# Attention inside a gated mix: three turns a head instead of four, sixteen exponential tiles, v kept 29 columns wide

## The chip, the core and the metric

One core of a Trainium2 chip. The metric is the device time of the whole kernel, in microseconds (us): the median of several runs. A profile of one execution, with every instruction of every engine and its start, comes with it.

## The reference

One block of 2048 tokens, 448 wide, goes through attention with 16 heads of 28 columns and through a gated feed-forward layer, and the two results are mixed by a gate per token. All in float32.

```python
x = A_x
g = _sigmoid((x * gate_w).sum(-1, keepdims=True))
# attention
qkv = (x @ wqkv).reshape(B, S, 3, H, Dh) ...
scores = jnp.einsum("bhqd,bhkd->bhqk", q, k) * (Dh ** -0.5)
p = _softmax(scores, axis=-1)
a = jnp.einsum("bhqk,bhkd->bhqd", p, v) ... @ wo
# feed-forward
b = (_gelu(x @ w_gate) * (x @ w_up)) @ w_down
return g * a + (1 - g) * b
```

S = 2048, D = 448, H = 16, Dh = 28; the hidden width F is 1792.

## The kernel before

**Precision.** A float32 product is taken as three products of parts (hi and lo of each operand, in the format float32r). The contraction over 448 rows so becomes 11 matmuls, the list `PAIRS`. q, k, the projections and the feed-forward layer work in this way; scores stack the parts of q and k on 114 rows, so that one matmul does; values are plain float32, which takes two passes, so that a profile shows two instructions for each.

**Stages.** First q, k, v and the gate's logits. Then attention, which is where the change lies. Then the feed-forward layer ("geglu") with the output projection mixed in.

**Attention.** For a head `h` and a tile `kt` of 128 keys, `scores` (L254) writes two score tiles of 128 keys x 1024 queries, `half` 0 and 1, each by two matmuls of 512 columns, into one of three buffers `sc`; ScalarE takes the exponentials into a tile `pt` of the pool `pp` (L261). `values` (L264) then multiplies v's tile of those keys into `po`: four matmuls of 512 queries, on four strips of 32 columns of TensorE's array side by side, twice for the two passes. `V` holds for each key tile and head 28 columns of v and 4 columns of ones; the first of these gives the sum of the exponentials. When a head is done, `finish` (L273) copies `po` out on VectorE (L275), sends the sums through memory to form reciprocals (L277 to L285), multiplies (L287) and stores (L289).

TensorE doesn't go to the values after every key tile. `ENDS` names the key tiles of a head after which it turns: it then writes `LATE` = 3 more score tiles (of what follows) and after that does the values of all the key tiles gathered. With `ENDS = (3, 7, 11, 15)` a turn has 4 key tiles, so 8 score tiles, and a head has 4 turns.

**Filling.** Between score tiles TensorE works on x @ w_up, and on a part of x @ w_gate, which the next stage will read: the generator `up` (L292) gives one matmul ("product") at a time, 17 weight tiles x 4 blocks of tokens x 11 = 748 in all. A block of 11 gathers in the only buffer `pu`; VectorE copies it to `u` (L307, two buffers), and a DMA stores it in `ud`. `fill(n)` (L315) issues up to n products, and after a block's last one none until two more score tiles are out (`hold`) or until the values have been done. The loop calls it after each score tile but two:

```python
                    if due and count == LATE:
                        for a in due:
                            values(*a)
                        due, hold = [], 0
                    elif count != LATE - 1 or h + kt == 0:
                        first, last = h == 0 and kt <= ENDS[0] + 1, h == H - 1 and kt > ENDS[-2]
                        fill(4 if first or last else RATE)
```

`count` is the number of score tiles since the last turn of `ENDS`, and `RATE` is 2. Products left at the end run in a row behind the last values (L352).

**What sets the order.** All matmuls keep the order in which the program writes them. The other engines' instructions and the DMAs, which all go through SyncE's queue (SP), are put in an order by a planner at compile time; each engine and the queue then work in that order. Semaphores make them wait for their data and for the buffers that they reuse.

**Memory.** `kq` holds Q and K of two heads, even and odd ones in turn. The pool `gp`, with the tiles of w_down (`draw` and `w`, L370 to L374), has room of its own on the other side of the memory from before the attention on, so the first of these tiles are loaded and split while the first heads run. The pools of the last stage (`ap`, `hp`, `tp`, `wpo`) take the addresses that the attention leaves.

Of the kernel before, what the change touches and what calls it, by code (L numbers as in the profile page):

```python
# [7 lines left out]
F32 = mybir.dt.float32  # L8
# [7 lines left out]

S, D, H, DH, F = 2048, 448, 16, 28, 1792
P = 128
TB = 512                 # tokens of a block
NTB = S // TB  # L20
NT = S // P              # token tiles
NKT = S // P             # key tiles
NQK = 2 * D // P         # row tiles of q and k together
NF = F // P              # tiles of the hidden width
FC = 2                   # hidden tiles of a chunk
ENDS = (3, 7, 11, 15)    # key tiles after which TensorE turns from scores to values
LATE = 3                 # score tiles that it writes before it turns
RATE = 2                 # products of x @ w_up, w_gate between score tiles
NB = 3                   # hidden tiles whose x @ w_gate is taken there, too
ORDER = (2, 3, 1, 4, 0, 5, 6)   # chunks of the hidden width  # L30
NR = 4 * DH + 2          # rows of a score product
VW = 450                 # v, the gate's column, a zero column
SCALE = DH ** -0.5
BOUND = 20.0             # scores within +-BOUND need no search for their maximum

# A float32 product is taken as hi*hi + lo*hi + hi*lo, where x = hi + lo exactly and both parts fit
# float32r. The contraction over 448 rows is cut into tiles 0..2 of 128 rows and 64 more rows, whose
# hi and lo parts share one tile. Pairs are (tile of x's parts, tile of the weight's parts).
PAIRS = [(b, w) for b in range(3) for w in (b, 4 + b)] + [(4 + b, b) for b in range(3)] + [(3, 3), (3, 7)]


# [1 line left out]
def gated_mix(ctx: ExitStack, tc: tile.TileContext, xT, wqk, wvg, wg, wu, wd, wo, sel, ident, out):  # L43
    nc = tc.nc

    def mm(o, lhsT, rhs, start, stop):
        tc.keep_in_program_order(nc.tensor.matmul(o, lhsT, rhs, start=start, stop=stop))  # L47

    dram = ctx.enter_context(tc.tile_pool(name="dram", bufs=1, space=DRAM))
    qkd = dram.tile([2, 2 * D, S], F32, name="qkd")      # hi, lo of q's and k's rows  # L50
    shd = dram.tile([H, 2, S], F32, name="shd")          # hi, lo of minus the rows' shifts
    od = dram.tile([D, S], F32, name="od")                # attention outputs, by head rows
    dend = dram.tile([H, S], F32, name="dend")            # softmax denominators
    rdend = dram.tile([H, S], F32, name="rdend")          # their reciprocals
    ud = dram.tile([NF + NB, P, S], F32, name="ud")       # x @ w_up and some of x @ w_gate

    keep = ctx.enter_context(tc.tile_pool(name="keep", bufs=1))
    X = keep.tile([P, 7, S], F32R, name="X")
    gate = keep.tile([P, 3, NT], F32, name="gate")        # logits, g, 1 - g
    fw = ctx.enter_context(tc.tile_pool(name="fw", bufs=2))  # L60
    attn = ctx.enter_context(ExitStack())
    vp = attn.enter_context(tc.tile_pool(name="vp", bufs=1))
    V = vp.tile([P, NKT, H, 32], F32, name="V")
    kq = attn.enter_context(tc.tile_pool(name="kq", bufs=1))
    heads = [tuple(kq.tile([NR, S], F32R, name=f"{x}{i}") for x in "QK") for i in range(2)]
    for _, K in heads:
        nc.gpsimd.memset(K[96:].bitcast(F32), 1.0)
    nc.gpsimd.memset(V[:, :, :, DH:], 1.0)

# [1 line left out]
    with ExitStack() as ph:  # L71
        wp = ph.enter_context(tc.tile_pool(name="wp", bufs=1))
        st = ph.enter_context(tc.tile_pool(name="st", bufs=2))
# [8 lines left out]

        def raw(src, n=TB):
            t = st.tile([P, TB], F32, name="raw", bufs=6)[:, 0:n]
            nc.sync.dma_start(out=t, in_=src)
# [14 lines left out]
        def load_x(tb):  # L100
            s = slice(tb * TB, (tb + 1) * TB)
            rs = [raw(xT[tb, :, b]) for b in range(4)]
            for b in range(3):
                nc.scalar.activation(X[:, b, s], rs[b], AF.Copy)  # L104
            nc.gpsimd.tensor_copy(X[0:64, 3, s], rs[3][0:64])
            hr = st.tile([P, TB], F32R, name="xhr", bufs=1)
            nc.scalar.activation(hr[64:], rs[3][64:], AF.Copy)
# [5 lines left out]
        def qk_tile(t, tb):  # L113
            s = slice(tb * TB, (tb + 1) * TB)
            p = ps.tile([P, TB], F32, name="pqk")
# [27 lines left out]
            for t in range(NQK):  # L143
                qk_tile(t, tb)

        # |q.k| <= (sum of q's squared maxima + sum of k's) / 2, by head
        sq = wp.tile([P, NQK], F32, name="sq")
        nc.vector.tensor_reduce(sq, mx, axis=AX.X, op=OP.max)
        nc.vector.tensor_tensor(sq, sq, sq, OP.mult)
# [6 lines left out]
        for t in range(NQK):  # L156
            mm(pr[0:1, 0:H], sq[:, t:t + 1], selt[:, t], t == 0, t == NQK - 1)
        for i in range(4, NT):
            v_tile(i)
# [6 lines left out]
        for a in range(2):  # L166
            nc.vector.tensor_copy(sh[:, a, :], hcol[:, a:a + 1].bitcast(F32).to_broadcast([H, P]))
            nc.sync.dma_start(out=shd[:, a].rearrange("h (i n) -> h i n", n=P),
                              in_=sh[:, a:a + 1].to_broadcast([H, NT, P]))
        far = wp.tile([1, 2], F32, name="far")  # L170
# [1 line left out]
        nc.vector.tensor_reduce(far[:, 0:1], pr[0:1, 0:H], axis=AX.X, op=OP.max)  # L172
        nc.vector.tensor_scalar(far[:, 1:2], far[:, 0:1], 2.0 * BOUND / SCALE, None, OP.is_le)
        nc.vector.tensor_copy(flag, far[:, 1:2])
        # g = 1 / (1 + exp(-t))
        nc.scalar.activation(gate[:, 0], gate[:, 0], AF.Exp, scale=-1.0)
        nc.vector.tensor_scalar(gate[:, 0], gate[:, 0], 3e38, 1.0, OP.min, OP.add)  # L177
        nc.vector.reciprocal(gate[:, 1], gate[:, 0])  # L178
# [10 lines left out]
    load_k(heads[0][1], 0)  # L189
    load_q(heads[0][0], 0)  # L190

# [1 line left out]
    bounded = nc.values_load(flag[0:1, 0:1], min_val=0, max_val=1)  # L193
    with tc.If(bounded < 1):
        with ExitStack() as ph:
            gp = ph.enter_context(tc.tile_pool(name="gp", bufs=2))
# [4 lines left out]
            for h in range(H):  # L201
# [5 lines left out]
                for i in range(NT):  # L207
                    p = gps.tile([P, S], F32, name="gsc")
# [11 lines left out]
                nc.sync.dma_start(out=shd[h].rearrange("a (i n) -> i a n", i=NT),  # L220
                                  in_=ms.bitcast(F32))

    gp = ctx.enter_context(tc.tile_pool(name="gp", bufs=1, side="right"))
# [1 line left out]
    halves = {}  # L225

    def load_half(src, f, key, hi):
# [7 lines left out]
    def by_act(o, i):  # L235
        nc.scalar.activation(o, i, AF.Copy)

# [1 line left out]
    with ExitStack() as ph:  # L239
        pp = ph.enter_context(tc.tile_pool(name="pp", bufs=12))  # L240
        op = ph.enter_context(tc.tile_pool(name="op", bufs=2))
        psc = ph.enter_context(tc.tile_pool(name="psc", bufs=3, space=PSUM))
        pso = ph.enter_context(tc.tile_pool(name="pso", bufs=1, space=PSUM))
# [1 line left out]
        PT, PO = {}, {}  # L245
# [18 lines left out]
        def values(h, kt):  # L264
            if kt == 0:
                PO[h] = pso.tile([P, 512], F32, name="po")
            for j in range(4):
                mm(PO[h][j * 32:(j + 1) * 32], V[:, kt, h, :],
                   PT[h, kt, j // 2][:, (j % 2) * 512:(j % 2 + 1) * 512], kt == 0, kt == NKT - 1)
            if kt == NKT - 1:  # L270
                finish(h)
# [18 lines left out]
                                  in_=o[j * 32:j * 32 + DH])  # L290

        def up():  # L292
            # x @ w_up, a product at a time
            todo = [(wu, f, "u") for f in range(NF)] + [(wg, f, "g") for f in range(NB)]
            load_half(*todo[0], nc.vector.tensor_copy)
            for n, (_, f, key) in enumerate(todo):
                for tb in range(NTB):
                    if tb == 1 and n + 1 < len(todo):
                        load_half(*todo[n + 1], nc.vector.tensor_copy)
                    s = slice(tb * TB, (tb + 1) * TB)  # L300
                    p = psu.tile([P, TB], F32, name="pu")
                    for i, (x, w) in enumerate(PAIRS):
                        mm(p, halves[key, f][:, w], X[:, x, s], i == 0, i == len(PAIRS) - 1)
                        if i < len(PAIRS) - 1:
                            yield False
                    u = op.tile([P, TB], F32, name="u")
                    nc.vector.tensor_copy(u, p)  # L307
                    nc.sync.dma_start(out=ud[n, :, s], in_=u)
                    yield True
# [3 lines left out]
        hold = 0  # L313

        def fill(n):  # L315
            # up to n products, and after a block's last none before two more score tiles
            nonlocal hold
            while n and not hold:
                n -= 1
                if next(filler, None):  # L320
                    hold = 2
# [9 lines left out]
        for h in range(H):  # L331
            for kt in range(NKT):
                if kt == 2 and h + 1 < H:
                    load_head(h + 1)
                for half in range(2):
# [6 lines left out]
                    elif count != LATE - 1 or h + kt == 0:  # L342
                        first, last = h == 0 and kt <= ENDS[0] + 1, h == H - 1 and kt > ENDS[-2]
# [9 lines left out]
            pass  # L353
    attn.close()

# [1 line left out]
    with ExitStack() as ph:  # L357
        ap = ph.enter_context(tc.tile_pool(name="ap", bufs=1, reuse_waits="tile"))
        acc = ap.tile([P, NT, D], F32, name="acc")
        hp = ph.enter_context(tc.tile_pool(name="hp", bufs=2, reuse_waits="tile"))  # L360
        tp = ph.enter_context(tc.tile_pool(name="tp", bufs=3, reuse_waits="tile"))
        wpo = ph.enter_context(tc.tile_pool(name="wpo", bufs=1, reuse_waits="tile"))
        psg = ph.enter_context(tc.tile_pool(name="psg", bufs=3, space=PSUM, reuse_waits="tile"))
        psd = ph.enter_context(tc.tile_pool(name="psd", bufs=5, space=PSUM, reuse_waits="tile"))
# [47 lines left out]
                    nc.vector.scalar_tensor_tensor(y, p, g1, acc[:, t], OP.mult, OP.add)  # L412
                    nc.sync.dma_start(out=out[0, t * P:(t + 1) * P], in_=y)

        # the output projection of a block of tokens, mixed in
        WO = wpo.tile([P, 8, D], F32R, name="WO")
        OHL = {}

# [87 lines left out]
```

## Time and profile before

| | us |
|---|---|
| runs, median of 3 (lowest, highest) | 1068.43 (1067.9, 1068.51) |
| profiled execution, span | 1068.0 |
| first stage, to the first scores | 0 to 124 |
| attention, to the last product of the filling | 124 to 777.3 |
| geglu and output projection | 777.3 to 1068.0 |
| TensorE busy, whole span | 1054.2 |
| ScalarE busy, whole span | 616.8 |
| VectorE busy, whole span | 320.2 |

The engines are called PE (TensorE's matmuls), PEld (its weight loads), DVE (VectorE), ACT (ScalarE), POOL (GpSimd) and SP (SyncE, the DMA queue) in the profile's rows. A row of a group has the line of the program, the engine, the operation, what it writes and reads, and a count; then busy time, mean time of one in ns, and idle time before them with what ended it. A row of the timeline has start and length in us, and joins equal instructions that follow each other. All matmuls have line L47, since one helper issues them: `sc`, `po`, `pu`, `pg`, `pd` tell them apart by what they write. A row of a stage's windows has its ends, its length, then busy time and count of PE, PEld, DVE, ACT and POOL, and the clock granted to TensorE (1.00 here).

### The profile page before, as it was taken

The page shows a single profiled execution, that of the slowest core. Times are in us where ns is not written, and L with a number is a line of the kernel's source. Part 1 is how long each engine was busy: PE and PEld are TensorE (multiplying, and loading weights), DVE is VectorE, ACT ScalarE, POOL GpSimd, SP SyncE. Part 2 cuts the span into 40 slices and gives each one's busy share as a digit, 9 for nine tenths or more (in the row PEclk, how much of TensorE's full clock was granted, in tenths as well). Part 3 has the DMA queues.
Part 4 walks back from the last instruction along what each step waited for, and adds up shares of the span by engine and source line. Part 5 has one row for each costly group of instructions (what it writes and reads, how often), then busy time and mean ns, then how long its engine had stood idle before and what let it go on. Part 6 is the DMA issues. An engine that isn't in the chain of part 4 may idle for free.

```text
span 1068.0 us, 14546 instructions
## 1 busy us (share of the span) xinstructions
PE 1054.2 (99%) x5664; PEld 732.2 (69%) x5664; DVE 320.2 (30%) x519; ACT 616.8 (58%) x732; POOL 41.5 (4%) x32
## 2 busy tenths in 40 slices
PE   7999999999999999999999999999999999999998
PEld 5789756556556556556556566565588888888887
DVE  5561111111111111110110110110156656577555
ACT  6322478778777777777777787787643332233321
POOL 5300000000000000000000000000001011100000
PEclk9999999999999999999999999999999999999999
DMA  8875122332332332342332332331164323342233
GB/s 267 291 258 145 57 75 73 120 103 73 102 103 74 98 107 73 94 112 73 94 112 73 93 111 73 94 102 41 64 191 142 99 86 91 95 148 67 63 87 115
DMA packets 58907, 115.85 MB, mean 108 GB/s; under 512 B 12784, under 2 KB 18160, under 8 KB 55216
## 3 DMA queue, kind: packets, MB, share of 16 engines
q1 hardware_dynamic: 58832, 114.85, 35.8%
q8 instruction: 47, 0.77, 0.3%
q14 instruction: 28, 0.23, 0.1%
HBM read 74.44 MB, written 40.37 MB: 108 GB/s over the span
## 4 chain that ended last, share of the span: by engine, by line
PE 88%; DVE 0%; issue 0%; DVEq 0%
PE sc L47 23%; PE po L47 21%; PE pd L47 16%; PE pu L47 16%; PE pg L47 11%; DVE u L307 0%; DVE y L412 0%; DVE gate L178 0%; DVE gate L177 0%; DVE gate L179 0%; DVEq L307 0%
## 5 line engine op out<-in xcount | busy, mean ns | idle before, releaser
L261 ACT ACTIVATE pt<-sc 128x1024 f32<-128x1024 f32 x512 | 482.4, 1026 | 164.6 <-PE sc L47 163.9
L47 PE MATMUL sc<-Q,K 114*128 114x512 f32 x1024 | 317.9, 402 | 1.3 <-issue 1.3
L47 PEld LDWEIGHTS sc<-Q,K 114*128 114x128 f32 x1024 | 188.8, 189 | 94.3 <-issue 54.5
L47 PE MATMUL pu<-X,half 128*128 128x512 f32 x748 | 237.8, 397 | 0.4 <-DVE u L307 0.3
L47 PE MATMUL po<-pt,V 128*32 128x512 f32 x2048 | 233.0, 595 | 0.0
L307 DVE COPY u<-pu 128x512 f32<-128x512 f32 x68 | 47.0, 691 | 491.6 <-PE pu L47 484.7
L47 PEld LDWEIGHTS pu<-X,half 128*128 128x128 f32 x748 | 141.0, 189 | 35.9 <-issue 1.4
L47 PEld LDWEIGHTS po<-pt,V 128*32 128x32 f32 x2048 | 60.0, 109 | 137.8 <-issue 132.2
L47 PE MATMUL pd<-w,hl 128*128 128x448 f32 x672 | 140.9, 366 | 0.0
L47 PEld LDWEIGHTS pd<-w,hl 128*128 128x128 f32 x672 | 126.2, 188 | 12.2
L47 PE MATMUL pg<-X,half 128*128 128x512 f32 x484 | 116.6, 395 | 0.0
L47 PEld LDWEIGHTS pg<-X,half 128*128 128x128 f32 x484 | 90.7, 187 | 20.9
L47 PE MATMUL pqk<-X,WQK 128*128 128x512 f32 x308 | 75.0, 404 | 7.7 <-ACT X L104 6.0
L47 PEld LDWEIGHTS pqk<-X,WQK 128*128 128x128 f32 x308 | 58.6, 192 | 23.7 <-ACT X L104 6.9
L389 ACT ACTIVATE g<-pg 128x512 f32<-128x512 f32 x44 | 26.2, 595 | 78.7 <-PE pg L47 78.6
L390 DVE TENSOR_TENSOR g<-g,u 128x512 f32<-128x512 f32 x56 | 46.0, 830 | 55.0 <-ACT g L389 55.0
L391 ACT ACTIVATE hl<-g 128x512 fp32r<-128x512 f32 x56 | 35.2, 630 | 42.4 <-DVE g L390 36.6
L409 DVE SCALAR_TENSOR_TENSOR acc<-pd,gate,acc 128x448 f32<-128x448 f32 x80 | 53.0, 679 | 6.8 <-PE pd L47 6.8
L437 POOL TENSOR_TENSOR ohl<-oraw,ohl 128x1536 fp32r<-128x1536 f32 x4 | 14.0, 3511 | 752.0 <-DMA u<-ud 749.2
L392 DVE TENSOR_TENSOR hl<-g,hl 128x512 fp32r<-128x512 f32 x56 | 38.3, 687 | 10.6 <-ACT hl L391 8.7
L47 PE MATMUL pd<-WO,ohl 128*128 128x448 f32 x176 | 37.0, 368 | 0.0
L47 PE MATMUL pv<-WV,X 128*128 128x450 f32 x176 | 36.4, 366 | 0.0
(60 smaller groups left out, 325.1 us busy)
## 6 DMA issues: line engine op xcount, KB each, us to landing
ud<-u SPq DMA_DIRECT2D x68, 256.0 KB
qkd<-hl SPq DMA_DIRECT2D x28, 512.0 KB
Q<-qkd SPq DMA_DIRECT2D x64, 224.0 KB
K<-qkd SPq DMA_DIRECT2D x64, 224.0 KB
u<-ud SPq DMA_DIRECT2D x56, 256.0 KB
raw<-in_xT SPq DMA_DIRECT2D x16, 256.0 KB
rb<-rdend SPq DMA_DIRECT2D x64, 64.0 KB
hraw<-in_wu SPq DMA_DIRECT2D x14, 256.0 KB
```

The lines of the kernel that those rows point to most:

```text
L47: tc.keep_in_program_order(nc.tensor.matmul(o, lhsT, rhs, start=start, stop=stop))
L261: nc.scalar.activation(pt, sc, AF.Exp, scale=SCALE)
L307: nc.vector.tensor_copy(u, p)
L389: nc.scalar.activation(g, pg, AF.Gelu_apprx_tanh)
L390: nc.vector.tensor_tensor(g, g, u, OP.mult)
L391: nc.scalar.activation(hl[:, 0], g, AF.Copy)
L392: nc.vector.tensor_tensor(hl[:, 1], g, hl[:, 0].bitcast(F32), OP.subtract)
L409: nc.vector.scalar_tensor_tensor(acc[:, t], p, g1, acc[:, t], OP.mult, OP.add)
L437: nc.gpsimd.tensor_tensor(O[:, 4:7], o[:, 0:3], O[:, 0:3].bitcast(F32), OP.subtract)
```

## The change

`ENDS` becomes `(5, 10, 15)`: three turns a head, of 6, 5 and 5 key tiles. The pool `pp` of exponential tiles grows from 12 to 16. To make room for it, `V` is kept with 29 columns a head (28 of v and one of ones) instead of 32, with three columns of zeros behind the last head; the values' matmuls still take 32 columns, and the three beyond the 29 now belong to the next head and fall on rows of `po` that nobody reads. `gp` loses its own room: it is opened, with `tp` and `hp`, at the start of the last stage on the addresses of Q, K and V. `kq` and `vp` change places.

```diff
-ENDS = (3, 7, 11, 15)    # key tiles after which TensorE turns from scores to values
+ENDS = (5, 10, 15)
...
+VC = DH + 1
...
-    vp = attn.enter_context(tc.tile_pool(name="vp", bufs=1))
-    V = vp.tile([P, NKT, H, 32], F32, name="V")
     kq = attn.enter_context(tc.tile_pool(name="kq", bufs=1))
     heads = [tuple(kq.tile([NR, S], F32R, name=f"{x}{i}") for x in "QK") for i in range(2)]
+    vp = attn.enter_context(tc.tile_pool(name="vp", bufs=1))
+    VA = vp.tile([P, NKT, H * VC + 3], F32, name="V")
+    V = VA[:, :, 0:H * VC].rearrange("p k (h d) -> p k h d", h=H)
...
     nc.gpsimd.memset(V[:, :, :, DH:], 1.0)
+    nc.gpsimd.memset(VA[:, :, H * VC:], 0.0)
...
-    gp = ctx.enter_context(tc.tile_pool(name="gp", bufs=1, side="right"))
...
-        pp = ph.enter_context(tc.tile_pool(name="pp", bufs=12))
+        pp = ph.enter_context(tc.tile_pool(name="pp", bufs=16))
...
-                mm(PO[h][j * 32:(j + 1) * 32], V[:, kt, h, :],
+                mm(PO[h][j * 32:(j + 1) * 32], VA[:, kt, h * VC:h * VC + 32],
                    PT[h, kt, j // 2][:, (j % 2) * 512:(j % 2 + 1) * 512], kt == 0, kt == NKT - 1)
...
     with ExitStack() as ph:
+        gp = ph.enter_context(tc.tile_pool(name="gp", bufs=1, reuse_waits="tile"))
+        tp = ph.enter_context(tc.tile_pool(name="tp", bufs=3, reuse_waits="tile"))
+        hp = ph.enter_context(tc.tile_pool(name="hp", bufs=2, reuse_waits="tile"))
         ap = ph.enter_context(tc.tile_pool(name="ap", bufs=1, reuse_waits="tile"))
         acc = ap.tile([P, NT, D], F32, name="acc")
-        hp = ph.enter_context(tc.tile_pool(name="hp", bufs=2, reuse_waits="tile"))
-        tp = ph.enter_context(tc.tile_pool(name="tp", bufs=3, reuse_waits="tile"))
```

## The prediction

> **What bounds the kernel now.** I read the page first: busy shares, slices, chain.
>
> ```profile
> span 1068.0 us, 14546 instructions
> PE 1054.2 (99%) x5664; PEld 732.2 (69%) x5664; DVE 320.2 (30%) x519; ACT 616.8 (58%) x732; POOL 41.5 (4%) x32
> PE   7999999999999999999999999999999999999998
> ACT  6322478778777777777777787787643332233321
> PE sc L47 23%; PE po L47 21%; PE pd L47 16%; PE pu L47 16%; PE pg L47 11%; DVE u L307 0%; DVE y L412 0%; DVE gate L178 0%; DVE gate L177 0%; DVE gate L179 0%; DVEq L307 0%
> ```
>
> TensorE has work in every slice, and the chain is made of its matmuls: scores (sc), values (po), and x @ w_up (pu, "products" below) in the attention stage. ScalarE stands at 0.7 to 0.8 in that stage, so it is second, but not far behind. Since TensorE is never without work, the question is how much dead time the change takes out of its stream or puts into it. A busy row hides gaps under about 0.16 us (a matmul is drawn 0.40 long but starts each 0.23), so I read starts, in the timeline of TensorE over two turns:
>
> ```profile
> 506.87 1.11 PE L47 MATMUL sc<-Q,K 114*128 114x512 f32 x4
> 507.91 3.64 PE L47 MATMUL po<-pt,V 128*32 128x512 f32 x32
> 511.48 0.74 PE L47 MATMUL sc<-Q,K 114*128 114x512 f32 x2
> 512.06 0.62 PE L47 MATMUL pu<-X,half 128*128 128x512 f32 x2
> 512.52 0.63 PE L47 MATMUL sc<-Q,K 114*128 114x512 f32 x2
> 512.99 0.63 PE L47 MATMUL pu<-X,half 128*128 128x512 f32 x2
> 513.45 0.63 PE L47 MATMUL sc<-Q,K 114*128 114x512 f32 x2
> ...
> 516.72 0.40 PE L47 MATMUL pu<-X,half 128*128 128x512 f32 x1
> 516.96 1.08 PE L47 MATMUL sc<-Q,K 114*128 114x512 f32 x4
> 517.96 3.64 PE L47 MATMUL po<-pt,V 128*32 128x512 f32 x32
> ...
> 528.05 2.35 PE L47 MATMUL po<-pt,V 128*32 128x512 f32 x20
> ```
>
> Weight loads and ScalarE inside the first visit:
>
> ```profile
> 508.36 0.13 PEld L47 LDWEIGHTS po<-pt,V 128*32 128x32 f32 x4 [0.30 <-issue]
> ...
> 510.51 0.13 PEld L47 LDWEIGHTS po<-pt,V 128*32 128x32 f32 x4 [0.30 <-issue]
> ...
> 512.32 1.03 ACT L261 ACTIVATE pt<-sc 128x1024 f32<-128x1024 f32 x1 [2.57 <-PE sc L47]
> ```
>
> Four matmuls (two scores, two products) take 513.45 - 512.52 = 0.93, so one takes 0.233. Values come in groups of four: six groups from 508.36 to 510.51 are five steps, 0.43 each; a visit has 32/4 = 8. Two turns take 528.05 - 507.91 = 20.14, one 10.07. Its work is 16 + 11 = 27 matmuls x 0.233 = 6.29 and 8 x 0.43 = 3.44, together 9.73. The other **0.34** is what going to values and back costs.
>
> **Part 1, fewer turns: -5.4 us.** 64 visits become 48; work per head is the same. 16 x 0.34 = 5.4 (bounds from the rounding of the steps: 4.3 to 6.6). The Trainium skill, "TensorEngine Tiling (Array Packing)", Tiling Modes, Key Properties, states that changing the tiling mode drains TensorE; by that alone the change gains, here 5.4, and the trace agrees with 0.34 a visit. It says nothing of what the longer turns do to the filling, which the next parts price.
>
> **Part 2, the filling loses step: +5.2.** fill gives two products after score tile 1 and after tiles 4 to n of a turn: for n = 8 six calls, 12 places. A block has 11 products, so each turn holds one, and its last falls on tile 1 of the next turn, just ahead of the values: the DVE copy out of the only psu buffer runs beside the values. After the change turns have n = 12, 10, 10, with 20, 16, 16 places, and blocks end anywhere. A block's end then uses 14 places for 11 products (one cut off, one call skipped by hold). Going through the loop call by call, the turns get: the first 44 products; 24 turns of n = 10 get 13, 6 get 12; of n = 12, 9 get 17, 3 get 16, 3 get 14; the last two 15 and 18. That is 704 of 748, and 50 times the next block starts after exactly two score tiles, once a turn. The head of the stage shows what this costs, since it fills that way now:
>
> ```profile
> 128.73 0.39 PE L47 MATMUL pu<-X,half 128*128 128x512 f32 x1
> 128.96 1.09 PE L47 MATMUL sc<-Q,K 114*128 114x512 f32 x4
> 129.16 0.69 DVE L307 COPY u<-pu 128x512 f32<-128x512 f32 x1 [3.85 <-PE pu L47]
> 129.90 0.53 PEld L47 LDWEIGHTS pu<-X,half 128*128 128x128 f32 x3 [0.28 <-DVE u L307]
> 129.90 1.20 PE L47 MATMUL pu<-X,half 128*128 128x512 f32 x4
> 131.41 1.09 PE L47 MATMUL pu<-X,half 128*128 128x512 f32 x4
> ```
>
> And the list of waits over the stage (total, times, longest):
>
> ```profile
> PEld pu L47 <- DVE u L307: 1.3, 3, 0.7
> PEld sc L47 <- ACT pt L261: 0.6, 2, 0.4
> ```
>
> The copy ends at 129.85, the weight load it releases starts at 129.90, which is when TensorE would have gone on anyway (128.96 + 4 x 0.233 = 129.89); but the load was not done ahead, so the four products take 1.20 instead of 1.09: 0.11. The list of waits has 3 of these before; 47 more x 0.11 = **5.2**. Below: 0, if copies come in time. Above: a copy that queues behind another VectorE piece adds up to its length; VectorE is busy 13% of the stage (row below), so 50 x 0.13 x 0.35 = 2.3 more.
>
> ```profile
> 124.00:777.30 653.30, 653.01 (x3809) 387.89 (x3810) 87.16 (x149) 484.75 (x517) 0.00 (x0) 1.00 0.31 90
> ```
>
> **Part 3, ScalarE becomes the pace in parts: +7.5.** The score buffer is three tiles deep, so the third late tile (3') waits for the exp of tile n. Where TensorE waits on exp is seen twice now, in the turns in which ScalarE also prepares a w_down tile:
>
> ```profile
> 200.77 0.57 ACT L373 ACTIVATE w<-draw 128x448 fp32r<-128x448 f32 x1
> 201.23 4.67 ACT L261 ACTIVATE pt<-sc 128x1024 f32<-128x1024 f32 x5
> 204.50 1.05 PE L47 MATMUL sc<-Q,K 114*128 114x512 f32 x3
> 205.04 0.30 PEld L47 LDWEIGHTS sc<-Q,K 114*128 114x128 f32 x2 [0.35 <-ACT pt L261]
> ```
>
> A backlogged exp takes (4.67 - 1.03)/4 = 0.91; three scores need 1.05 where 0.63 + 0.23 = 0.86 is usual, so that wait cost 0.19. In a long turn, counted from its first score: ScalarE frees 3' at 0.84 (511.48 to 512.32) + (n-4) x 0.91 + 1.03 + 0.05 release + 0.10 lost load. TensorE is there at 0.11 (slow first score) + (n-1) x 0.466 + 0.11 + 0.233 x products. Both are equal at 17.0 products for n = 12 and 13.2 for n = 10; for n = 8 (without the second 0.11) at 9.8, under the 11 that it has. So a turn with 14 of 17 waits 3 x 0.233 = 0.70 (x3), 16 waits 0.23 (x3), 12 of 13.2 waits 0.28 (x6): 2.1 + 0.7 + 1.7 = 4.5. The 33 turns that just balance wait 0 to 0.15, since TensorE at 0.93 a tile paces ScalarE up to the block's end and its later tiles come in a rush; 0.09 x 33 = 3. Together **7.5** (bounds 3 to 9.5: the three groups without their lost loads, and the 33 at 0.15). The Trainium skill, "Trainium Kernel Development and Optimization", Performance Expectations, calls matmul busy time a bad metric and the share of weight loading a good one. By it TensorE (69%) would have room to hide such waits; that is rival A.
>
> **Part 4, four blocks at the end: +3.1.** 748 - 704 = 44 products are left behind the last values, where 11 are now:
>
> ```profile
> 774.63 2.83 PE L47 MATMUL pu<-X,half 128*128 128x512 f32 x11
> 777.31 10.43 PE L47 MATMUL pg<-X,half 128*128 128x512 f32 x44
> ```
>
> They run with nothing between them. From a block's last product to the next block: 0.43 (128.73 to 129.16) + 0.69 + 0.05 + 0.10 = 1.27 instead of 0.23; three such gaps x 1.04 = **3.1**. Below: 2.8, without the lost load. Above: the third and fourth copies reuse the two u buffers, whose stores stand in SP's queue among those of the last head; +3.
>
> **At nothing:** the POOL memset of v's ones gets smaller and one is added; POOL's next piece waits for x anyway:
>
> ```profile
> 7.92 1.14 POOL L105 CAST X<-raw 64x512 fp32r<-64x512 f32 x1 [2.62 <-DMA raw<-in_xT]
> ```
>
> Values' weights at a step of 29: the same 32 columns; no row shows the address's effect, but 0.30 of 0.43 between loads is free, so they could triple. Sixteen exp tiles: a turn holds 12 + 3, as 8 + 3 of 12. The w_down tiles (gp), until now loaded and split inside the first heads, lie after the change on Q and K of the even heads, free from head 14's end; their three loads move past the SP queue of fourteen heads, and their ScalarE and VectorE pieces under the last turns and the 44 products (13 us, where 2.6 stood). If one falls among exps, it costs the 0.19 above, as now. First geglu inputs get more time ahead, not less.
>
> **Sum:** -5.4 + 5.2 + 7.5 + 3.1 = **+10.4** on the profiled span of 1068.0, which is 0.4 under the median 1068.43 of the runs: 1078.8.
>
> **Rivals.** *A, faster:* the waits are absorbed, because copies and exps arrive within the time the weight loads are ahead. Then -5.4 + 3.1 = -2.3: 1066.1. For it: before, TensorE's stream has almost no such wait. Against: the 129.90 row, with the very spacing of the new turns. It decides below (5.4 - 3.1)/48 = 0.05 a turn for both waits. *B, no change:* only one of the two waits is real, the other swallowed by it (a TensorE that waits 0.11 for psu gives ScalarE that time): -5.4 + 3.1 + 4.5 = +2.2 with the 4.5 alone, and under that if part 2 eats of it: 1070. *C, worse:* VectorE's order, planned before the run, puts o x rb (L287, which needs a chain of four DMA steps) ahead of a u copy; in each turn the product behind it and all scores wait. A wait of 1 us in each of 16 heads gives 1095. Before, reciprocal and product stand behind copies and find their data landed, but blocks ended at fixed places then.
>
> **Chances.** Forecast 0.70 (1072 to 1084); A 0.07; B 0.12; C 0.11. Two tenths of a per cent (2.1 us) is about what runs here can tell from no change: faster 0.07, same 0.10, slower 0.83. The range goes from B to the upper bounds with part of C: 1070 to 1086.
>
> **What would show it.** Visits to values 48, each 10 or 12 groups at 0.43. In the waits, loads of pu behind DVE u about 50 times with small times, loads of sc behind ACT pt some 40 times. Behind the last values 44 products with three gaps of 1 us. ScalarE's pauses at values 48 instead of 64, each longer (about 2.57 + 0.86 or 1.72, less the backlog). If loads of pu find the copy done, part 2 falls; if exps run under 0.85 when backlogged, part 3 does. If the groups of values change from 0.43, v's layout matters after all: 256 key tiles x 2 groups x each 0.01 is 5 us.

## The result, and the profile after

The changed kernel takes 1096.01 us (median of 4 runs, 1095.39 to 1097.03) against 1068.47 of the kernel before in the same runs: ratio 1.0257, 95% interval 1.0242 to 1.0271. It is 27.5 us slower; 10.4 were forecast, and the time lies outside the stated range (1070 to 1086).

The page of the changed kernel, the parts that answer to those shown of before:

```profile
span 1095.1 us, 14538 instructions
PE 1064.1 (97%) x5664; PEld 727.2 (66%) x5664; DVE 321.7 (29%) x519; ACT 614.0 (56%) x732; POOL 40.5 (4%) x33
PE   7999999999999799999999999999999999999998
PEclk9999999999999899999999999999999999999999
PE 80%; issue 3%; ACT 2%; DVE 1%; DMA 1%; SPq 1%; DVEq 0%; ACTq 0%
```

The chain was 88% TensorE's; now it goes through ScalarE, VectorE, a DMA and SyncE's queue as well, and one slice in the attention has TensorE at 0.7 with a lower clock. By the windows, the attention stage (to the first pg, the next stage's first product) takes all of it:

```profile
124.00:806.20 682.20, 664.62 (x3810) 383.50 (x3811) 88.21 (x150) 481.77 (x517) 0.00 (x0) 0.99 0.31 87
806.20:1095.20 289.00, 284.93 (x1333) 249.76 (x1331) 180.16 (x267) 89.53 (x142) 16.47 (x8) 1.00 0.35 106
```

682.2 stands where 653.3 stood (+28.9; the first scores came 0.7 later). The rest has 289.0, where the same stretch of before, 777.3 to its end, has 290.7. The list of waits has what TensorE, and VectorE for its copies, waited for (total, times, longest):

```profile
PEld pu L48 <- DVE u L309: 32.5, 54, 7.9
DVE u L309 <- DMA ud<-u: 28.6, 5, 6.1
PEld sc L48 <- ACT pt L263: 16.8, 48, 0.6
PE pu L48 <- DVE u L309: 15.8, 10, 7.5
```

A waiting load is not yet lost time: it normally runs 0.23 ahead of its matmul. But the counts are near those that the prediction named: 54 loads of pu behind a copy where about 50 were named, 48 of sc behind an exponential where some 40 were. What it did not forecast is the 7.9. TensorE's rows around it:

```profile
352.72 0.40 PE L48 MATMUL pu<-X,half 128*128 128x512 f32 x1
352.96 1.12 PE L48 MATMUL sc<-Q,K 114*128 114x512 f32 x4
361.53 1.22 PE L48 MATMUL pu<-X,half 128*128 128x512 f32 x2 [7.45 <-DVE u L309]
364.39 5.98 PE L48 MATMUL po<-pt,V 128*32 128x512 f32 x40
370.30 0.73 PE L48 MATMUL sc<-Q,K 114*128 114x512 f32 x2
```

VectorE and SyncE's queue in the same microseconds:

```profile
353.17 0.43 DVE L233 CAST half<-hraw 128x512 fp32r<-128x512 f32 x1 [11.23 <-PE pu L48]
353.63 0.69 DVE L234 TENSOR_TENSOR half<-hraw,half 128x512 fp32r<-128x512 f32 x1
354.24 0.68 DVE L289 TENSOR_TENSOR o<-o,rb 128x512 f32<-128x512 f32 x1
354.95 1.60 SPq L291 DMA_DIRECT2D od<-o  x4
357.32 0.82 SPq L310 DMA_DIRECT2D ud<-u  x2
360.79 0.69 DVE L309 COPY u<-pu 128x512 f32<-128x512 f32 x1 [5.87 <-DMA ud<-u]
```

Read it from below. The copy of u at 360.79 needs the u buffer of two blocks before, so the landing of that block's store. Two stores, this one and the next, had stood in SyncE's queue until 357.32, behind od (the attention's output) and two loads; od waits for o x rb; o x rb stands on VectorE behind the cast of a new weight tile (its data were asked for from 343.38 on, and at 564.96 such data landed 4.7 us after their request); and the cast had sat there for 11.23 us, until TensorE's last product with the tile whose buffer it reuses (352.72). That product is also the last of a block. So the copy that empties pu comes behind everything that was itself waiting for the block's end. TensorE stands for 7.5 us, and then works at half clock (the third figure from the end in these windows, before and after the pause):

```profile
340.00:353.00 13.00, 12.97 (x81) 7.16 (x80) 0.85 (x2) 8.73 (x10) 0.00 (x0) 1.00 0.20 58
361.50:367.00 5.50, 5.47 (x22) 2.46 (x26) 0.00 (x0) 1.94 (x2) 0.00 (x0) 0.50 0.13 53
```

Five other copies are late in this way or a shorter one. At 454, 496 and 540 the cast and the subtraction merely go ahead of the copy, at a cost of 1.1 each:

```profile
454.11 0.43 DVE L233 CAST half<-hraw 128x512 fp32r<-128x512 f32 x1 [10.57 <-PE pu L48]
454.57 0.69 DVE L234 TENSOR_TENSOR half<-hraw,half 128x512 fp32r<-128x512 f32 x1
455.18 0.68 DVE L309 COPY u<-pu 128x512 f32<-128x512 f32 x1
```

At 413 it is the whole chain again (1.8), with the values standing in most of its time. At 572 it is the store alone (1.4), and no cast stands ahead: o x rb waited for its own data, and the stores stood behind od.

```profile
564.96 0.69 DVE L289 TENSOR_TENSOR o<-o,rb 128x512 f32<-128x512 f32 x1 [6.12 <-DMA rb<-rdend]
565.68 1.60 SPq L291 DMA_DIRECT2D od<-o  x4
568.07 0.82 SPq L310 DMA_DIRECT2D ud<-u  x2
571.48 0.69 DVE L309 COPY u<-pu 128x512 f32<-128x512 f32 x1 [5.83 <-DMA ud<-u]
572.23 0.73 PE L48 MATMUL pu<-X,half 128*128 128x512 f32 x2 [1.29 <-DVE u L309]
578.24 0.74 PE L48 MATMUL sc<-Q,K 114*128 114x512 f32 x2
```

Taking the excess of the starts over 0.233, the six hold TensorE 7.6 + 1.8 + 3 x 1.1 + 1.4 = 14.1 us. The slow clock costs 2.8 more: from 361.53 to 370.30 TensorE needs 8.77 for two products, four scores and a visit of ten groups, where the same work from 572.23 to 578.24 takes 6.01. The four blocks behind the last values are as forecast, 3.61 from start to start instead of 11 x 0.233 = 2.56:

```profile
796.30 2.82 PE L48 MATMUL pu<-X,half 128*128 128x512 f32 x11 [0.78 <-DVE u L309]
799.91 2.82 PE L48 MATMUL pu<-X,half 128*128 128x512 f32 x11 [0.78 <-DVE u L309]
803.52 2.83 PE L48 MATMUL pu<-X,half 128*128 128x512 f32 x11 [0.78 <-DVE u L309]
```

### The profile page after: what moved, and what is told of

Its sections match the earlier page's. It is cut to its first block, busy times and chain, and to the rows that moved or that the text cites. A ratio compares the mean times of both kernels' runs of the same rounds, so it can differ in the third digit from the quotient of the medians.

```text
span 1095.1 us, 14538 instructions
## 1 busy us (share of the span) xinstructions
PE 1064.1 (97%) x5664; PEld 727.2 (66%) x5664; DVE 321.7 (29%) x519; ACT 614.0 (56%) x732; POOL 40.5 (4%) x33
## 4 chain that ended last, share of the span: by engine, by line
PE 80%; issue 3%; ACT 2%; DVE 1%; DMA 1%; SPq 1%; DVEq 0%; ACTq 0%
PE po L48 20%; PE sc L48 20%; PE pd L48 16%; PE pu L48 14%; PE pg L48 10%; ACT pt L263 2%; DMA ud<-u 1%; DVE u L309 1%; SPq L291 0%; DMA rb<-rdend 0%; DVE half L233 0%; DVE o L289 0%; DVE half L234 0%; DMA rdend<-r 0%; SPq L186 0%
## 5 line engine op out<-in xcount | busy, mean ns | idle before, releaser
L48 PE MATMUL pu<-X,half 128*128 128x512 f32 x748 | 240.4, 404 | 16.0 <-DVE u L309 15.8
L48 PEld LDWEIGHTS sc<-Q,K 114*128 114x128 f32 x1024 | 186.4, 190 | 94.8 <-issue 41.0
L48 PEld LDWEIGHTS pu<-X,half 128*128 128x128 f32 x748 | 137.1, 189 | 62.4 <-DVE u L309 32.5
L277 DVE COPY o<-po 128x512 f32<-128x512 f32 x16 | 11.1, 692 | 108.8 <-PE po L48 108.8
```

Source lines behind the costliest of these rows:

```text
L277: nc.vector.tensor_copy(o, PO[h])
```

## The experiments

The first four ran together on one chip, beside runs of the kernel before with a median of 1069.71; the last three on another, beside 1068.55. Differences of times between the two sets, or with the changed kernel's own runs (beside 1068.47), are therefore uncertain by about 1 us.

**Four turns, all else of the change kept.**

```diff
-ENDS = (5, 10, 15)
+ENDS = (3, 7, 11, 15)
```

> The changed kernel with four turns again (ENDS 3, 7, 11, 15), all the rest of the change kept: v 29 columns wide, 16 exponential tiles, the pools in their new places. Theory (the loss is in the longer turns: filling out of step, late copies): the time of before, 1068.5, within 1067 to 1070, and no late copies. Rival (v's columns or the moved pools cost): most of the 27 stays, over 1080; the groups of values would then last other than 0.43 us each.

Measured 1067.83, ratio to before 0.9988 (0.9978 to 0.9998). Its list of waits is nearly that of before:

```profile
PEld pu L48 <- DVE u L309: 1.3, 3, 0.7
PEld sc L48 <- ACT pt L263: 0.3, 1, 0.3
```

So v at 29 columns, the sixteen tiles and the moved pools cost nothing in a kernel of four turns; a gain of 0.1% is too small to rest anything on. All of the loss comes with the three turns.

**The splitting behind the copy.**

```diff
-                        load_half(*todo[n + 1], nc.vector.tensor_copy)
+                        with tc.issue_after(last.ins):
+                            load_half(*todo[n + 1], nc.vector.tensor_copy)
...
-                    nc.vector.tensor_copy(u, p)
+                    last = nc.vector.tensor_copy(u, p)
```

> The changed kernel, with VectorE's splitting of the next weight tile queued behind the copy of u that the program writes just before it. Theory (six copies of u are late because this splitting, planned ahead of them, waits for TensorE's last product; o x rb and so SyncE's stores stand behind it): the six waits of 1.1 to 7.6 us (14 us together) and the slow clock after the longest (2 us) go: 1080, within 1077 to 1083, which is what the forecast's own terms without its rival C give. Rival (SyncE's queue is late of itself): the waits of 7.6, 1.8 and 1.4 stay, 1090 or more.

Measured 1082.6 (1080.49 to 1085.1), ratio 1.0117 (1.0101 to 1.0134): 13.4 under the changed kernel. Its list of waits:

```profile
DVE u L310 <- DMA ud<-u: 22.0, 4, 5.6
PEld pu L48 <- DVE u L310: 19.7, 53, 1.4
PE pu L48 <- DVE u L310: 3.9, 6, 0.9
```

Copies still wait for stores (22.0 in 4 waits, up to 5.6), but TensorE's longest wait for a copy falls from 7.9 to 1.4. That one has no cast ahead: like the copy at 572, it waits for a store behind od, and o x rb had waited 6.0 for its own data.

```profile
559.32 0.69 DVE L310 COPY u<-pu 128x512 f32<-128x512 f32 x1 [5.59 <-DMA ud<-u]
560.06 0.73 PE L48 MATMUL pu<-X,half 128*128 128x512 f32 x2 [0.95 <-DVE u L310]
```

So the rival, that SyncE's queue is late of itself, fails for the waits of 7.6 and 1.8, which are gone though no buffer was added and no store moved by hand; for the short one it holds. The edit moved the cast, but the planner then laid out the rest anew, so the cast's share isn't measured by itself.

**Four u buffers.**

```diff
-        pp = ph.enter_context(tc.tile_pool(name="pp", bufs=16))
+        pp = ph.enter_context(tc.tile_pool(name="pp", bufs=15))
...
-                    u = op.tile([P, TB], F32, name="u")
+                    u = op.tile([P, TB], F32, name="u", bufs=4)
```

> The changed kernel with four u buffers instead of two and 15 exponential tiles instead of 16. Here a copy of u no longer needs the store of two blocks before. Theory: the three waits that ended on such a store (7.6, 1.8, 1.4 us) and the slow clock go, the three of 1.1 behind the splitting stay unless the plan changes: 1083, within 1080 to 1086. Rival (SyncE's stores are not the cause of the long ones): 1094 to 1097.

Measured 1079.15 (1078.55 to 1080.39), ratio 1.009 (1.0073 to 1.0107): 4 less than expected and under the expected range, since the planner also laid VectorE's work out anew. None of the casts ahead of a copy is left (at 525.4 TensorE waits 0.20 and 0.23 for a cast and its subtraction that come behind their copy); so this run doesn't separate the two halves of the chain. No copy waits for a store any more:

```profile
PEld pu L48 <- DVE u L309: 18.0, 52, 1.2
PEld sc L48 <- ACT pt L263: 16.3, 50, 0.6
PE pu L48 <- DVE u L309: 2.6, 4, 0.8
```

1096.0 - 1079.2 = 16.9 is about the price of the late copies and their slow clock; by the starts it was 14.1 + 2.8 = 16.9. It is a kernel near the forecast's likeliest case (1078.8), and serves to test that case's terms from here on.

**Shorter exponentials**, on the kernel with the splitting behind the copy.

```diff
-            nc.scalar.activation(pt, sc, AF.Exp, scale=SCALE)
+            nc.scalar.activation(pt[:, 0:960], sc[:, 0:960], AF.Exp, scale=SCALE)
...
-                   PT[h, kt, j // 2][:, (j % 2) * 512:(j % 2 + 1) * 512], kt == 0, kt == NKT - 1)
+                   PT[h, kt, j // 2][:, (j % 2) * 448:(j % 2) * 448 + 512], kt == 0, kt == NKT - 1)
```

> As the kernel with the splitting behind the copy, but exponentials of 960 of each 1024 queries only (the values take overlapping slices of 512, TensorE's work is unchanged). Leaves out 64 queries of each 1024. Theory (in the longer turns TensorE waits for exponentials, 7 to 8.5 us): 6 us under the kernel with the splitting behind the copy, so 1074, and the loads of sc that wait for ScalarE fall from 48 to under 15. Rival (ScalarE has time enough, the dead time is TensorE's own at the turns and blocks): the same time as that kernel within 1 us.

Measured 1074.06 (1073.44 to 1074.19), 8.5 under 1082.6 where 6 were expected, with TensorE's instructions the same. The waits for ScalarE, 18.1 in 53 before the edit, are nearly gone, at 15 where under 15 were expected:

```profile
PEld sc L48 <- ACT pt L263: 3.3, 15, 0.3
PE pu L48 <- DVE u L310: 5.3, 6, 1.4
```

The second row was 3.9 in 6 waits before the edit: copies cost 1.4 more here, so the exponentials themselves are worth nearer 10. An engine that is busy 57% of the span costs 8.5 us or more; that it is because the turns ask for it in rushes fits the next experiment, in which the waits for it halve. The rival is refuted.

**Even filling**, on the kernel with four u buffers.

```diff
-        hold = 0
+        hold, owed = 0, 0.0
 
         def fill(n):
             nonlocal hold
             while n and not hold:
                 n -= 1
                 if next(filler, None):
                     hold = 2
+            return n
+
+        def even(n):
+            nonlocal owed
+            owed = min(owed + n, 4 + n)
+            k = min(int(owed), 4)
+            owed -= k - fill(k)
...
-                        fill(4 if first or last else RATE)
+                        even(4 if first or last else 1.7)
```

> The kernel with four u buffers, and a filling that makes up for what hold left out: 1.7 products after a score tile, and up to 4 at once while it is behind. Every turn then gets its share (44 a head) and no block is left at the end. Theory (ScalarE's waits come from turns short of products, and the four left blocks cost 3 us): 8.5 us under the kernel with four u buffers (1079.2), so 1070.7, within 1069 to 1073; loads of sc that wait for ScalarE from 50 to under 25, loads of pu that wait for the copy stay near 50. Rival (three turns cost ScalarE's time whatever the filling is): no more than the 3 us of the left blocks, 1076.

Measured 1069.6 (1068.3 to 1070.17), ratio 1.0005 (0.9995 to 1.0014): some 9 us under the kernel with four u buffers (9.6 by the times, 9.1 by the ratios to the kernel before), level with the kernel before, in three turns.

```profile
PEld pu L48 <- DVE u L309: 15.3, 54, 0.7
PEld sc L48 <- ACT pt L263: 7.9, 32, 0.4
```

ScalarE's waits halve (32 times, where under 25 were expected), no block is left at the end (TensorE goes from the last values straight to pg), and the lost loads stay, as they should. What three turns cost hangs on how they are filled.

**Short copies**, on the kernel with four u buffers.

```diff
-                    nc.vector.tensor_copy(u, p)
-                    nc.sync.dma_start(out=ud[n, :, s], in_=u)
+                    nc.vector.tensor_copy(u[:, 0:256], p[:, 0:256])
+                    nc.sync.dma_start(out=ud[n, :, s].rearrange("p (a n) -> p a n", a=2),
+                                      in_=u[:, None, 0:256].to_broadcast([P, 2, 256]))
```

> The kernel with four u buffers, and copies of u of 256 of the 512 columns (stored twice). Leaves out half of x @ w_up and of the part of x @ w_gate. The copies are about 0.27 us shorter, so the weight load behind them is in time. Additive theory (as in the forecast: lost loads 5.2 and ScalarE's waits are separate terms): 5.2 + 0.8 less, 1073. Coupled theory (the 0.11 that TensorE loses at a block's end is time that ScalarE gets; without it the turn waits for ScalarE instead): only 1 to 3 us less, 1076 to 1078, loads of pu that wait nearly gone, and the waits of sc for ScalarE longer in total by some 4 us.

Measured 1077.0 (1076.21 to 1077.6), ratio 1.0071 (1.005 to 1.0093): 2.1 under the kernel with four u buffers, as the coupled theory has it, and not 6. The intervals of the two ratios overlap (1.0073 to 1.0107 there), so that the 2.1 may be less; 6 is excluded.

```profile
PEld sc L48 <- ACT pt L263: 21.4, 50, 0.6
PEld pu L48 <- DVE u L309: 3.3, 4, 0.9
```

The 52 waits of loads for copies become 4, and the waits for ScalarE grow from 16.3 to 21.4. In a turn that lacks products, 0.11 lost at a block's end is time that ScalarE uses to catch up; take it away, and TensorE waits for ScalarE instead. The growth of 5.1 in those waits fits this; no run changes it alone.

**Even filling and short copies.** Both edits, on the kernel with four u buffers.

> Both: the even filling and the short copies, with four u buffers. Leaves out half of x @ w_up and of the part of x @ w_gate. If the three terms (late filling, lost loads, left blocks) are the whole loss, what stays is the gain of 16 turns less a few us of ScalarE's waits: 1067, within 1065 to 1069, under the kernel before. If something else costs in three turns: over 1070.

Measured 1065.38 (1064.89 to 1066.65), ratio 0.9967 (0.9955 to 0.9978): 3.2 us under the kernel before by the medians. With the filling even, short copies bring 1069.6 - 1065.4 = 4.2 instead of 2.1. The gain of sixteen fewer turns shows only here, in a kernel that leaves out half of the filling's results; no kernel of three turns with whole copies was faster than the one before.

## Why the prediction was wrong

Direction and place were right: slower, all of it in the attention, through the filling and ScalarE. The size was not, since the largest loss came by a way to which the prediction gave 2.3 us at most. By its own steps:

- **Part 1** (-5.4) holds as a term. A visit of the changed kernel, in the timeline:

```profile
342.19 5.36 PE L48 MATMUL po<-pt,V 128*32 128x512 f32 x48
347.48 0.73 PE L48 MATMUL sc<-Q,K 114*128 114x512 f32 x2
```

  From its start to the next score are 5.29 = 12 x 0.43 + 0.13; before it was 511.48 - 507.91 = 3.57 = 8 x 0.43 + 0.13. So this 0.13, a part of the 0.34, is the same in a longer visit, and there are 16 visits fewer. With most of the other losses taken out the kernel ends 3.2 under the one before.
- **Part 2** (+5.2) had the right count, 54 waits of which 50 were forecast. The failed step is its upper bound: "a copy that queues behind another VectorE piece adds up to its length; VectorE is busy 13% of the stage", 2.3 us. It took VectorE's other work as falling at random and costing its own length. But the cast waits for the same event as the copy, so they meet at every fourth block's end; and VectorE, which works in order, was held by an instruction that waits (11.23 us for the cast), not only by one that runs. The two u buffers were priced at +3 above part 4, for the last blocks alone, where no copy waited for a store; it was inside the stage that they cost. Late copies and their slow clock came to some 17 us (1096.0 to 1079.2), beside the lost loads.
- **Rival C** was this, half seen: it put o x rb ahead of a copy through its own DMAs, in all heads, at 1 us each, with a chance of 0.11. That its 1095 is so near to 1096 is luck. What stood in front was the cast in five of the six late copies, in two of them with o x rb and the stores behind it; only at 572 had o x rb waited for its own DMAs, and even there the copy was late through the store. The six cost 1.1 to 7.6 us each. The rows of before had the pieces of this, though not the order:

```profile
507.07 0.69 DVE L307 COPY u<-pu 128x512 f32<-128x512 f32 x1 [9.21 <-PE pu L47]
507.68 0.42 DVE L231 CAST half<-hraw 128x512 fp32r<-128x512 f32 x1
508.74 0.69 DVE L287 TENSOR_TENSOR o<-o,rb 128x512 f32<-128x512 f32 x1
512.28 0.82 SPq L308 DMA_DIRECT2D ud<-u  x2
719.91 0.69 DVE L307 COPY u<-pu 128x512 f32<-128x512 f32 x1 [6.86 <-DMA ud<-u]
```

  Here, too, cast and o x rb run at the block's end, but behind the copy, and two stores of u go out together, 4.5 us after the later copy. At 719.91 a copy even waits 6.86 for a store. It cost nothing because the copy stood beside the values (from 719.43), as at nearly every block's end, and the next block's end was 10 us off in most turns. The prediction asked what VectorE's share was and not what else waits for the block's end.
- **Part 3** (+7.5, bounds 3 to 9.5): shorter exponentials took 8.5 away, nearer 10 with the copies that were later in that run. Right in kind, and at its upper bound or a little above.
- **Part 4** (+3.1): three gaps of 3.61 - 2.56 = 1.05 where 1.04 was forecast. Right.
- **At nothing**: v's columns, the tiles and the pools, shown for four turns (0.9988).
- **Rival A** falls: the waits were not absorbed, whatever room a share of 66% to 69% for weight loading seemed to leave. With the late copies gone the kernel was still 9.4 above the one before (1079.15 against 1069.71). **Rival B**'s coupling fits what was measured (short copies brought 2.1 instead of 6), but it works within parts 2 and 3 and doesn't bring the kernel level.
- **Luck**: the kernel with four u buffers lands on the forecast's 1078.8, but not with the forecast's terms. In it short copies were worth some 2 us, not 5.2, and in the kernel with the splitting behind the copy the exponentials were worth more than 7.5.

Not settled: how much of the 17 us is the order on VectorE and how much the two u buffers. Either edit takes most of it, which fits a chain that needs both, but the plan changed in both.

## What to carry to other kernels

When work that fills gaps is divided into blocks, the place where a block ends is a resource: a rhythm in which it always falls beside other long work hides its copy, its stores and whatever else waits for that event. Before stretching a loop, count what each turn then holds, and list all instructions that wait for the block's last matmul, on every in-order engine and queue, in their planned order. In this kernel waiting instructions on an engine busy 13% of the stage, and a queue behind them, cost 17 us.

## What was not expected of the hardware

After a pause of 7.5 us TensorE's granted clock was 0.50 for the next 5.5 us, and groups of values took 0.85 instead of 0.43; after the pauses of 1.6 and 1.3 us (413 and 572) it stayed at 1.00. The Trainium skill, "TensorE: Matmul & The Clock Gate", Why this matters for your kernels, warns of idle gaps over about 3 us between matmuls, after which the clock falls to half; this trace agrees on both kinds of pause, and the price here was 2.8 us. A wait of a weight load that ends just when the matmul is due costs 0.11 (1.20 for four products instead of 1.09), some fifty times a kernel here.
